# Full attention layers in 64x32 matmul tiles: two banks of values, two score tiles, values between the score pairs

## The chip, the cores and the metric

The kernel runs on one core of a Trainium2 chip. The metric is the device time of one execution in microseconds (us), the median of several runs. TensorE (PE, with its weight loads PEld) multiplies matrices into accumulation banks, VectorE (DVE), ScalarE (ACT) and GpSimd (POOL) work on rows of 128 partitions, SyncE (SP) issues transfers.

## What is computed

Four transformer layers without feed-forward parts, in the order A, B, A, B, each with layer norm and a residual sum. A is attention over a sliding window of 256, B is full attention. There are 2048 rows, 512 features, 32 heads of 16.

```python
qkv = (x @ wqkv).reshape(B, S, 3, H, Dh)          # B=1, S=2048, D=512, H=32, Dh=16
scores = einsum("bhqd,bhkd->bhqk", q, k) * Dh ** -0.5
# A only: where(0 <= i - j < 256, scores, -1e9)
o = einsum("bhqk,bhkd->bhqd", softmax(scores), v)
x = x + reshape(o) @ wo                            # x on the right is layer-normed first
```

## The kernel before

**Layers and loops.** Layers 0 and 2 are sliding layers, 1 and 3 full ones. `attention` goes over blocks of 512 queries (c, 4 of them) and over quarters of heads (qd, 8 quads of 4 heads); in this text one pass of `attn_full` over all keys for one c and qd is called a quarter. A quarter has 16 steps, one for each 128 keys (j). A full layer so has 32 quarters and 512 steps. In layer 3 the quarters come in the order of pairs of quads (t) first, then c.

**A step.** `exps` is called twice (pr 0 and 1). Each call makes the scores of two heads: two matmuls (L714) of 64 contraction rows (queries and keys lie there in float16 parts, with sums for the shift) by 128 key columns over 512 queries, into the two banks of a score tile. ScalarE then takes one exponential over both banks (L718, 128x1024), into one of six buffers `e`. Then `pv` of the step two before multiplies the exponentials by the values: four heads, each 128 rows by 17 columns (16 features and a column of ones, the denominator) in float32, written to the four 32-partition parts of one bank, `acc[0]` (L758). The compiled program has two matmul instructions for each of these.

**Score tiles.** The pool `ps_s` has two tiles of two banks. In full layers a third, `PH["third"]`, takes every third call.

**End of a quarter.** `epilogue` transposes the bank of values (VectorE, L686), keeps the least and the summed denominators, divides, and after every second quad transposes back and casts for the output projection (L689 to L702).

**Side work.** Projections of queries, keys and values, the output projection, and norms of later blocks run as generators (`Work`), in pieces of one 512-column matmul step (a "pass" below) between attention steps. The class `Side` hands them out: it keeps a modelled clock (`spent`), a budget per step (`share`), and a time `PH["free"]` before which no new tile is begun. A tile of side work is twelve passes (three in `wo_part`, layer 3), made by `mms`; in full layers each pass is four matmuls of 128 rows by 32 columns (L429) into one bank, `acc[1]`, which `bank()` returns. VectorE takes the result out of it: two operations for queries and keys (L527, L528), one for values (L638), one for output tiles (L652, L673). The squares of queries and keys are summed over heads by `squares` (L550) into the same bank and read by one operation. `finish` at the end of a block makes what is left, piece after piece.

**Order.** PE's instructions are issued in the order written (a manual schedule). The other engines' order is made by a scheduler with priorities (`high_priority` moves an instruction ahead). Values are queued in `pvq`; after each step `flush(2)` leaves two steps in it, then `sd.step()` gives the side its turn:

```python
pvq.append([f])
flush(2)
sd.step()
```

So PE's order in a step is: scores, scores, values of two steps before, side passes. Banks: two for `acc`, four for the score pool, two for the third tile, eight in all.

## Time and profile before

| | |
|---|---|
| runs | 2757.61 us median of 3 (2755.26 to 2764.16) |
| profiled execution | span 2759.8 us from first to last instruction; no other time is given for it |
| PE busy | 2636.2 us (96%) |
| ScalarE busy | 2377.0 us (86%) |
| VectorE busy | 956.6 us (35%) |
| GpSimd busy | 564.5 us (20%) |
| granted PE clock, mean | 0.992 |
| layer 1, layer 3 | 504 to 1456 us, 1789 to 2742 us (first to last exponential) |

How to read it. A row of groups has line, engine, operation, output and inputs by the program's names, count, then busy us, mean ns of one, and the engine's idle time before them with what ended it. A row of the timeline has start, length, engine, line, operation and count; a merged row covers several equal instructions. A row of stretches has start:end, length, and busy us (count) of PE, PEld, DVE, ACT and POOL, then granted clock, DMA share and GB/s. Matmuls are pipelined and their ends are modelled: distances of starts tell more than lengths. Slices of the page are a fortieth of the span each, digits are tenths.

### The profile page before, as it was taken

What the parts mean: (1) busy time and instruction counts of PE and PEld (TensorE: products, weight loads), DVE (VectorE), ACT (ScalarE), POOL (GpSimd) and SP (SyncE); (2) the same over time, 40 slices, a digit from 0 to 9 for tenths busy, and PEclk for the clock granted to TensorE, in tenths of its full rate; (3) what the DMA queues carried; (4) which work ended last, traced back from release to release, by engine and by line L of the source; (5) the groups of instructions that cost most, each with busy time, mean ns of one, the idle gap of its engine ahead of it and who ended that gap; (6) DMA issues with size and microseconds to landing.
All of it is one profiled execution on the core that took longest, in us unless ns stands there. A gap on an engine that the chain in (4) does not pass through costs nothing.

```text
span 2759.8 us, 59658 instructions
## 1 busy us (share of the span) xinstructions
PE 2636.2 (96%) x24358; PEld 782.5 (28%) x24358; DVE 956.6 (35%) x2059; ACT 2377.0 (86%) x2687; POOL 564.5 (20%) x1129
## 2 busy tenths in 40 slices
PE   8989999999999999999998898999999999999997
PEld 4333344322222222222223333522222222222221
DVE  7678765112131113112215676512222222222122
ACT  3566664799999999999995677399999999999997
POOL 2477672000000000000004677100000000000000
PEclk9999999999999999999999999999999999999999
DMA  6877676322232123212325464613333343333321
GB/s 222 218 251 222 197 229 186 123 71 88 86 102 88 62 82 108 85 60 91 103 67 177 146 190 131 184 62 105 110 112 122 120 123 101 102 110 114 98 95 56
DMA packets 317501, 344.78 MB, mean 125 GB/s; under 512 B 113056, under 2 KB 233376, under 8 KB 311200
## 3 DMA queue, kind: packets, MB, share of 16 engines
q1 hardware_dynamic: 317216, 340.86, 40.4%
q8 instruction: 193, 3.16, 0.5%
q14 instruction: 92, 0.75, 0.1%
HBM read 228.07 MB, written 96.99 MB: 118 GB/s over the span
## 4 chain that ended last, share of the span: by engine, by line
PE 74%; ACT 9%; DVE 6%; issue 5%; POOL 3%; DMA 3%; SPq 0%; ACTq 0%; DVEq 0%; POOLq 0%
PE acc L758 30%; PE s L714 19%; PE acc L429 10%; PE b L432 9%; ACT e L718 8%; PE acc L791 3%; PE bs L432 2%; POOL e L781 1%; DVE ot L686 1%; POOL e L784 1%; POOL wr L344 1%; DVE sp L528 0%; POOL w L346 0%; PE acc L550 0%; DMA kt<-kw 0%
## 5 line engine op out<-in xcount | busy, mean ns | idle before, releaser
L718 ACT ACTIVATE e<-s 128x1024 f32<-128x1024 f32 (+2 forms) x2432 | 2243.5, 1116 | 96.8 <-PE s L714 90.2
L758 PE MATMUL acc<-e,vt 128*17 128x512 f32 x8192 | 1078.0, 598 | 5.3 <-DVE ot L686 4.1
L714 PE MATMUL s<-qt,kt 64*128 64x512 f16 (+3 forms) x5504 | 780.5, 355 | 64.7 <-ACT e L718 41.8
L714 PEld LDWEIGHTS <-kt 64*128 64x128 f16 x5504 | 204.9, 94 | 818.1 <-issue 795.1
L784 POOL TENSOR_SCALAR_AFFINE_SELECT e<-e 128x256 f32<-128x256 f32 x512 | 226.5, 450 | 127.0 <-ACT e L718 126.4
L758 PEld LDWEIGHTS acc<-e,vt 128*17 128x17 f32 x8192 | 136.2, 95 | 379.5 <-issue 347.9
L686 DVE STREAM_TRANSPOSE ot<-acc 128x512 f32<-128x512 f32 x128 | 91.3, 714 | 387.9 <-PE acc L758 317.2
L702 POOL TENSOR_TENSOR oh<-o,oh 128x512 f16<-128x512 f32 x31 | 36.0, 1160 | 886.5 <-DVE oh L701 886.5
L781 POOL TENSOR_SCALAR_AFFINE_SELECT e<-e 128x256 f32<-128x256 f32 x448 | 197.7, 447 | 76.9 <-ACT e L718 74.8
L791 PE MATMUL acc<-e,vt 128*17 128x384 f32 (+2 forms) x2816 | 202.7, 394 | 6.0 <-POOL e L781 4.0
L432 PE MATMUL b<-xc,w 128*128 128x512 f16 x672 | 157.0, 384 | 8.4 <-DVE sp L528 6.9
L533 POOL TENSOR_TENSOR sq_h<-sp_h 128x512 bf16<-128x512 f16 x27 | 28.1, 1039 | 482.7 <-DVE sp_h L527 482.7
L527 DVE TENSOR_SCALAR sp<-acc,es 128x512 f16<-128x512 f32 x28 | 20.9, 748 | 288.5 <-PE acc L429 276.8
L527 DVE TENSOR_SCALAR sp_h<-acc,es 128x512 f16<-128x512 f32 x27 | 20.3, 751 | 286.5 <-PE acc L429 286.5
L525 ACT ACTIVATE sp<-b,es 128x512 f16<-128x512 f32 x56 | 38.5, 687 | 89.6 <-PE b L432 87.4
L429 PE MATMUL acc<-xc,w_h 128*32 128x512 f16 x1296 | 108.6, 379 | 2.3 <-DVE km L566 2.3
L533 POOL TENSOR_TENSOR sq<-sp 128x512 bf16<-128x512 f16 x28 | 29.1, 1039 | 396.5 <-DVE sp L527 396.5
L429 PE MATMUL acc<-xc,w 128*32 128x512 f16 x1344 | 108.9, 379 | 0.3
L638 DVE COPY vt<-acc 128x256 f32<-128x256 f32 (+1 forms) x36 | 18.5, 513 | 257.6 <-PE acc L429 257.6
L673 DVE TENSOR_TENSOR dx<-acc,gcol 128x512 f32<-128x512 f32 x60 | 41.5, 692 | 176.6 <-PE acc L429 176.6
L429 PE MATMUL acc<-wo,oh 128*32 128x512 f16 x1296 | 101.3, 379 | 0.0
L432 PEld LDWEIGHTS <-w 128*128 128x128 f16 x720 | 67.3, 99 | 105.6 <-issue 33.8
(167 smaller groups left out, 1808.2 us busy)
## 6 DMA issues: line engine op xcount, KB each, us to landing
kt<-kf SPq DMA_DIRECT2D x128, 512.0 KB
qt<-qs SPq DMA_DIRECT2D x128, 256.0 KB
xd<-x SPq DMA_DIRECT2D x96, 256.0 KB
x<-xd SPq DMA_DIRECT2D x96, 256.0 KB
w<-wd SPq DMA_DIRECT2D x20, 1024.0 KB
kt<-kw SPq DMA_DIRECT2D x64, 256.0 KB
qs<-sp SPq DMA_DIRECT2D x48, 256.0 KB
wo<-wd SPq DMA_DIRECT2D x12, 1024.0 KB
```

Source lines behind the costliest of these rows:

```text
L429: nc.tensor.matmul(ps[g:g + 32], a[:, g:g + 32], b, start=(i == 0), stop=(i == len(pairs) - 1), skip_group_check=True)
L432: nc.tensor.matmul(ps, a, b, start=(i == 0), stop=(i == len(pairs) - 1))
L527: nc.vector.tensor_scalar(sp[:, 0], ps, e, None, op0=ALU.mult)
L533: nc.gpsimd.tensor_tensor(sq, sp[:, 0], sp[:, 0], ALU.mult)
L673: nc.vector.tensor_tensor(d, ps, gcol[1], ALU.mult)
L686: nc.vector.transpose(ot.rearrange("p b r -> p (b r)"), a)
L714: nc.tensor.matmul(ps[:, h, s0:s0 + wd_], kt[R * h:R * h + R, pr, kc:kc + P], qt[R * h:R * h + R, pr, qc:qc + wd_], start=True, stop=True)
L718: nc.scalar.activation(e[:, :, w0:w1], ps[:, :, w0:w1], AF.Exp, scale=SCALE)
L758: nc.tensor.matmul(a[32 * h:32 * h + DH + 1, :], V[l, qd // 4, j // 8][:, j % 8, 4 * (qd % 4) + h, :], es_[h // 2][:, h % 2, :], start=(j ...
L781: nc.gpsimd.affine_select(v, v, pattern=[[0, 2], [-1, P]], compare_op=ALU.is_gt, fill=0.0, base=0, channel_multiplier=1)
L784: nc.gpsimd.affine_select(v, v, pattern=[[0, 2], [1, P]], compare_op=ALU.is_ge, fill=0.0, base=0, channel_multiplier=-1)
L791: nc.tensor.matmul(a[32 * h:32 * h + DH + 1, q * P:(q + nb) * P], V[l, (4 * c + j) // 4][:, j % 4, 4 * qd + h, :], es_[h // 2][:, h % 2, s ...
```

## The change

In full layers every matmul is made of tiles of 64 contraction rows by 32 columns.

- Scores: eight matmuls a pair instead of two, into the same two banks.
- Values: each head's 128 keys are split into two halves of 64, one into `acc[0]`, one into `acc[1]`; the epilogue transposes both banks and adds the halves.
- Side passes: the contraction is split into two halves, into the two banks of a tile `PH["pair"]`, which takes the banks of the third score tile. `joined` copies one half out and adds the other on VectorE; the old operations then read the sum. Values of the side work are joined at their destination.
- Score tiles: two.
- Order: values of two steps before are issued between a step's two score pairs, side passes after the second pair. In step 2 of each quarter, whose values are the first of the quarter, side passes come between the pairs and values at the end.
- The planner's modelled times for scores and values change (0.27 to 0.22, 1.0 to 0.88).

```diff
-    def bank():
+    def bank(halves=False):
         if PH["full"]:
-            return acc[1]
+            return PH["pair"] if halves else PH["pair"][:, 0, :]
...
                 for g in range(0, P, 32):
-                    nc.tensor.matmul(ps[g:g + 32], a[:, g:g + 32], b, start=(i == 0), stop=(i == len(pairs) - 1),
-                                     skip_group_check=True)
+                    for r in range(2):
+                        half = slice(R * r, R * r + R)
+                        nc.tensor.matmul(ps[g:g + 32, r], a[half, g:g + 32], b[half], start=(i == 0),
+                                         stop=(i == len(pairs) - 1), skip_group_check=True)
...
+    def joined(n, ps, rows=slice(0, P)):
+        if not PH["full"]:
+            return ps
+        j = vp.tile([P, QC], F32, name=f"j{n}", tag="dn", bufs=2)
+        with tc.high_priority(HEAD_START):
+            nc.vector.tensor_copy(j[rows], ps[rows, 0])
+            nc.vector.tensor_tensor(j[rows], ps[rows, 1], j[rows], ALU.add)
+        return j
...
+            ps = joined(f"{n}_{t}", ps)          # project; likewise in squares, wo, wo_part
...
+                if more is not None:             # values
+                    nc.vector.tensor_copy(to, more[:, part])
+                    nc.vector.tensor_tensor(to, fr, to, ALU.add)
...
             nc.vector.transpose(ot.rearrange("p b r -> p (b r)"), a)          # epilogue
+            if l % 2:
+                ou = vp.tile([P, QC // 32, 32], F32, name=f"ou{n}", tag="o", bufs=1)
+                nc.vector.transpose(ou.rearrange("p b r -> p (b r)"), acc[1])
+        if l % 2:
+            nc.vector.tensor_tensor(ot[:, :, :DH + 1], ot[:, :, :DH + 1], ou[:, :, :DH + 1], ALU.add)
...
-        ps = PH["third"] if PH["full"] and turn["s"] % 3 == 0 else ps_s.tile([P, 2, QC], F32, name=f"s{name}", tag="s")
+        ps = ps_s.tile([P, 2, QC], F32, name=f"s{name}", tag="s")
...
-            for h in range(2):
-                nc.tensor.matmul(ps[:, h, s0:s0 + wd_], kt[R * h:R * h + R, pr, kc:kc + P],
-                                 qt[R * h:R * h + R, pr, qc:qc + wd_], start=True, stop=True)
-        spent(0.27)
+            for g in range(0, P, 32 if PH["full"] else P):
+                for h in range(2):
+                    out_ = slice(g, g + 32) if PH["full"] else slice(0, P)
+                    nc.tensor.matmul(ps[out_, h, s0:s0 + wd_], kt[R * h:R * h + R, pr, kc + out_.start:kc + out_.stop],
+                                     qt[R * h:R * h + R, pr, qc:qc + wd_], start=True, stop=True,
+                                     skip_group_check=PH["full"])
+        spent(0.22 if PH["full"] else 0.27)
...
             for pr in range(2):                  # attn_full
+                if pr and j == 2:
+                    PH["side"]()
+                elif pr:
+                    flush(1)
                 es_.append(exps(f"{l}_{c}_{qd}_{j}_{pr}", kt[j // 8], qt, pr, [(j % 8 * P, 0, QC, 0)]))
...
                 for h in range(4):
-                    nc.tensor.matmul(a[32 * h:32 * h + DH + 1, :], V[l, qd // 4, j // 8][:, j % 8, 4 * (qd % 4) + h, :],
-                                     es_[h // 2][:, h % 2, :], start=(j == 0), stop=(j == NT - 1),
-                                     skip_group_check=True)
+                    for r in range(2):
+                        half = slice(R * r, R * r + R)
+                        nc.tensor.matmul(acc[r][32 * h:32 * h + DH + 1, :],
+                                         V[l, qd // 4, j // 8][half, j % 8, 4 * (qd % 4) + h, :],
+                                         es_[h // 2][half, h % 2, :], start=(j == 0), stop=(j == NT - 1),
+                                         skip_group_check=True)
+            if j == 2:
+                flush(1)
+            else:
+                PH["side"]()
             yield pv
...
                         pvq.append([f])          # attention
-                        flush(2)
-                        sd.step()
                         if win:
+                            flush(2)
+                            sd.step()
                             settle(False)
```

More of the change, by code (lines that the diff above doesn't have):

```diff
@@ L404, in phase @@
         PH["full"], PH["win"] = l is not None and l % 2 == 1, l is not None and l % 2 == 0
-        if PH["full"] or not PH["win"] and "pool" not in PH or l is None and PH.get("third"):
+        if PH["full"] or not PH["win"] and "pool" not in PH or l is None and PH.get("pair"):
             ps_x.close()
             PH["pool"] = ps_x.enter_context(tc.tile_pool(name=f"ps_x{l}", bufs=1 if PH["full"] else 2, space=bass.MemoryType.PSUM))
-            PH["third"] = PH["pool"].tile([P, 2, QC], F32, name=f"s{l}") if PH["full"] else None
-    def bank():
+            PH["pair"] = PH["pool"].tile([P, 2, QC], F32, name=f"s{l}") if PH["full"] else None
+    def bank(halves=False):
         if PH["full"]:
-            return acc[1]
+            return PH["pair"] if halves else PH["pair"][:, 0, :]
         turn["bank"] += 1
@@ L513, in project @@
         for t in range(NHT) if ht is None else (ht,):
-            ps = bank()
+            ps = bank(True)
             w0 = t * P if ht is None else 0
@@ L546, in squares @@
     def squares(n, sqs):
-        ph = bank()
+        ph = bank(True)
         for t, sq in sqs.items():
-            nc.tensor.matmul(ph[32 * t:32 * t + 32, :], hsum, sq, start=True, stop=True, skip_group_check=True)
-        return ph
+            if PH["full"]:
+                for r in range(2):
+                    half = slice(R * r, R * r + R)
+                    nc.tensor.matmul(ph[32 * t:32 * t + 32, r], hsum[half], sq[half], start=True, stop=True, skip_group_check=True)
+            else:
+                nc.tensor.matmul(ph[32 * t:32 * t + 32, :], hsum, sq, start=True, stop=True, skip_group_check=True)
+        return joined(n, ph, slice(0, P) if len(sqs) > 1 else quarters(*sqs))
     def quarters(ht):
@@ L623, in values @@
         for i in tiles:
-            ps = bank()[:, :D1 - D0]
+            ps = bank(True)
+            ps = ps[:, :, :D1 - D0] if PH["full"] else ps[:, :D1 - D0]
             if first:
@@ L628, in values @@
                 yield from mms(ps, [(xc[:, b, k, i * P:(i + 1) * P], w[:, k, a, :D1 - D0]) for k in range(NC) for a, b in TERMS], us=us)
-            src = ps.rearrange("p (h d) -> p h d", d=DH)
+            src, more = ((ps[:, r].rearrange("p (h d) -> p h d", d=DH) for r in range(2)) if PH["full"]
+                         else (ps.rearrange("p (h d) -> p h d", d=DH), None))
             for x, h in enumerate(halves if l % 2 else (None,)):
                 to = vt[:, i, :, :DH] if h is None else dst[h][:, i, :, :DH]
-                fr = src if h is None else src[:, x * HH:(x + 1) * HH]
-                if first:
+                part = slice(0, H) if h is None else slice(x * HH, (x + 1) * HH)
+                fr = src[:, part]
+                if more is not None:
+                    nc.vector.tensor_copy(to, more[:, part])
+                    nc.vector.tensor_tensor(to, fr, to, ALU.add)
+                elif first:
                     nc.vector.tensor_tensor(to, fr, first[2].rearrange("p (h d) -> p h d", d=DH), ALU.mult)
@@ L646, in wo @@
         for i in range(4):
-            ps = bank()
+            ps = bank(True)
             yield from mms(ps, [(O[l, c, t][:, a, i * P:(i + 1) * P], w[:, t, b, :]) for t in range(NHT) for a, b in TERMS])
@@ L650, in wo @@
             k = 4 * c + i
+            ps = joined(f"o{l}_{k}", ps)
             with tc.high_priority(HEAD_START):
@@ L667, in wo_part @@
         for i in range(4):
-            ps = bank()
+            ps = bank(True)
             yield from mms(ps, [(o[:, a, i * P:(i + 1) * P], w[:, b, :]) for a, b in TERMS])
@@ L672, in wo_part @@
             k = 4 * c + i
+            ps = joined(f"o3_{c}_{t}_{i}", ps)
             nc.vector.tensor_tensor(d, ps, gcol[1], ALU.mult)
@@ L722, in flush @@
         while len(pvq) > n:
-            spent(1.0)
+            spent(0.88 if PH["full"] else 1.0)
             for f in pvq.popleft():
@@ L757, in pv @@
                 for h in range(4):
-                    nc.tensor.matmul(a[32 * h:32 * h + DH + 1, :], V[l, qd // 4, j // 8][:, j % 8, 4 * (qd % 4) + h, :],
-                                     es_[h // 2][:, h % 2, :], start=(j == 0), stop=(j == NT - 1),
-                                     skip_group_check=True)
+                    for r in range(2):
+                        half = slice(R * r, R * r + R)
+                        nc.tensor.matmul(acc[r][32 * h:32 * h + DH + 1, :],
[4 more added lines that the diff above has]
+                flush(1)
+            else:
+                PH["side"]()
             yield pv
@@ L977, in attention @@
                     nxt = load(l, c, qd + 1) if qd + 1 in qds else None
-                    a = acc[qd % 2 if win else 0]
+                    a, PH["side"] = acc[qd % 2 if win else 0], sd.step
                     began = clock[0]
```

## The prediction

> **What bounds the kernel now.** I read the page first (engines and slices), then busy time by stretch, then the order of time inside the two full layers.

> ```profile
> span 2759.8 us, 59658 instructions
> PE 2636.2 (96%) x24358; PEld 782.5 (28%) x24358; DVE 956.6 (35%) x2059; ACT 2377.0 (86%) x2687; POOL 564.5 (20%) x1129
> PE   8989999999999999999998898999999999999997
> DVE  7678765112131113112215676512222222222122
> ACT  3566664799999999999995677399999999999997
> 504.00:1456.00 952.00, 941.27 (x9234) 224.14 (x9237) 184.26 (x426) 946.76 (x1024) 47.48 (x46) 1.00 0.27 83
> 1789.00:2742.00 953.00, 935.94 (x8761) 229.55 (x8759) 220.54 (x436) 944.96 (x1024) 45.44 (x42) 1.00 0.33 103
> ```

> The full layers are the two stretches of 952 and 953 us with 1024 exponentials each (512 steps of two). PE, VectorE and ScalarE stand there at 941, 184 and 947 us of 952: two engines are full, VectorE is four fifths idle. The sliding layers, the other 855 us, keep their instructions; the change cannot move them but at their ends. Which of the two full engines sets the pace is read from the order of time.

> ```profile
> 1076.05 0.92 PE L714 MATMUL s<-qt,kt 64*128 64x512 f16 x4
> 1076.89 1.05 PE L758 MATMUL acc<-e,vt 128*17 128x512 f32 x8
> 1077.88 0.92 PE L714 MATMUL s<-qt,kt 64*128 64x512 f16 x4
> 1079.71 0.92 PE L714 MATMUL s<-qt,kt 64*128 64x512 f16 x4
> 1161.38 0.60 PE L714 MATMUL s<-qt,kt 64*128 64x512 f16 x4
> 1161.92 1.05 PE L758 MATMUL acc<-e,vt 128*17 128x512 f32 x8
> 1162.79 0.61 PE L429 MATMUL acc<-wv,xc 128*32 128x512 f16 x8
> 1163.34 0.61 PE L714 MATMUL s<-qt,kt 64*128 64x512 f16 x4
> 1167.03 0.61 PE L714 MATMUL s<-qt,kt 64*128 64x512 f16 x4
> 1168.55 0.61 PE L714 MATMUL s<-qt,kt 64*128 64x512 f16 x4
> 1169.95 0.83 PE L429 MATMUL acc<-wv,xc 128*32 128x512 f16 x12
> 1170.71 0.61 PE L714 MATMUL s<-qt,kt 64*128 64x512 f16 x4
> ```

> Where no side work runs, score groups come every 1.83 us (1076.05, 1077.88, 1079.71) and PE waits inside them (0.84 us to the values, against 0.54 at 1161.38): this is ScalarE's own pace, 0.917 us for one exponential. Packed by PE, a step is 1.52 us without side passes (1167.03 to 1168.55), 1.96 with two (1161.38 to 1163.34), and a third adds 0.21 (0.76 from 1169.95 against 0.55 from 1162.79). So ScalarE is the floor, and PE passes it only in steps of two passes or more. The floor is 512 x 1.833 = 938.7 us a layer; the stretches hold 952 and 953, together some 27 over it, 2 of them first and last edges. **25 us is all that a faster PE can win.**

> **The parts.** Inside a step, scores to values cost 0.54 us where two 512-column pairs need 2 x 0.21, and the last pass to the next scores 0.34 (0.55 for two passes less 0.21): each of the two changes of tile shape costs 0.12 us or so. With all tiles 64x32 both go. PE then needs 2 x 0.21 + 0.87 (1161.92 to 1162.79) + 0.21 a pass: 1.71 with two passes, 0.12 under the floor. In the built order some 110 steps of three passes are left (1.92 us), mostly beside steps of none or one. So the 25 us may go, as far as nothing new comes.

> Work per instruction: a score pair becomes eight matmuls, a value group sixteen, a side pass eight; matmul instructions grow from 24,358 by about 26,000. Moved columns per tile stay 512, so if eight tiles run side by side as four do now, no stream gets longer. No row shows a 64x32 tile. The lower bound is 0: a pass of four tiles and a pair of two 64x128 tiles both take 0.21. The upper is 0.04 us a score pair, a third of a shape change. I take the lower, to which the rows of four tiles are nearest, and keep the upper for the range. The fetch of instructions doubles from a small share.

> ```profile
> q8 instruction: 193, 3.16, 0.5%
> L714 PEld LDWEIGHTS <-kt 64*128 64x128 f16 x5504 | 204.9, 94 | 818.1 <-issue 795.1 <-DMA kt<-kw 5.0 <-DMA qs<-sp_h 0.6
> 1162.36 0.12 PEld L429 LDWEIGHTS <-xc 128*32 128x32 f16 x4 [0.31 <-issue]
> ```

> Weight loads: a 128-column load takes 94 ns, and four 32-column loads stand in 0.12 us, so they run beside each other; I charge nothing. [...]

> **Two score tiles, values between the pairs.** ScalarE's chain through PE is now closed over two tiles.

> ```profile
> 1463.92 1.02 ACT L718 ACTIVATE e<-s 128x1024 f32<-128x1024 f32 x1
> 1464.99 0.34 PE L714 MATMUL s<-qt,kt 64*128 64x384 f16 x2 [0.43 <-ACT e L718]
> 1999.05 0.61 PE L429 MATMUL acc<-xc,w_h 128*32 128x512 f16 x8 [0.77 <-DVE km L566]
> 1999.59 0.61 PE L714 MATMUL s<-qt,kt 64*128 64x512 f16 x4
> 2000.09 3.89 ACT L718 ACTIVATE e<-s 128x1024 f32<-128x1024 f32 x4 [1.54 <-PE s L714]
> ```

> An exponential lasts 1.02 us unqueued, scores follow its end by 0.05 (1464.94 to 1464.99), an exponential follows the scores' start by 0.50. First pair, values, second pair: 0.05 + 0.21 + 0.87 + 0.50 + 1.02 = 2.65, and one more exponential, 0.917, gives 3.57 for two steps of 3.67. The spare is 0.1, where the third tile gave nearly a whole exponential. Normal steps still fit. At the end of a quarter the side passes go between the pairs of step 2 and the values after them, so two value groups stand round one score pair: 2 x (0.21 + 0.87) = 2.16 between the second pairs of steps 2 and 3, 0.33 over the floor. Of this the spare covers 0.1, and an earlier start up to 0.16 (the tile is free 0.97 after the exponential before, where PE usually comes at 1.13), less where side passes stand in between: 0.07 to 0.17 is left. I take 0.14, since nearly every step 2 has passes: 64 x 0.14 = 9 us (between 5 and 11). Each longer wait below also delays the other tile by 0.16 (1.08 from pair to pair, less 0.917), 25 times or 4 us, and I put the three-pass steps at 0.04 each, 4 us (0.09 over the floor, less what the spare leaves). Together 17 us.

> **VectorE, and who waits.** These rows price what it gets.

> ```profile
> L686 DVE STREAM_TRANSPOSE ot<-acc 128x512 f32<-128x512 f32 x128 | 91.3, 714 | 387.9 <-PE acc L758 317.2 <-PE acc L791 69.6
> L673 DVE TENSOR_TENSOR dx<-acc,gcol 128x512 f32<-128x512 f32 x60 | 41.5, 692 | 176.6 <-PE acc L429 176.6
> L638 DVE COPY vt<-acc 128x512 f32<-128x512 f32 x12 | 8.3, 692 | 128.2 <-PE acc L429 128.2
> L527 DVE TENSOR_SCALAR sp<-acc,es 128x512 f16<-128x512 f32 x28 | 20.9, 748 | 288.5 <-PE acc L429 276.8
> L528 DVE SCALAR_TENSOR_TENSOR sp<-acc,es,sp 128x512 f16<-128x512 f32 x28 | 21.0, 750 | 0.9
> 1069.15 0.72 DVE L686 STREAM_TRANSPOSE ot<-acc 128x512 f32<-128x512 f32 x1 [10.25 <-PE acc L758]
> 1069.92 0.13 PEld L758 LDWEIGHTS acc<-e,vt 128*17 128x17 f32 x8 [0.58 <-DVE ot L686]
> 1070.60 0.43 DVE L696 TENSOR_TENSOR op<-ot,r 128x256 f32<-128x256 f32 x1
> ...
> 1159.36 0.71 DVE L699 STREAM_TRANSPOSE o<-op 128x512 f32<-128x512 f32 x1
> 1160.11 0.43 DVE L701 CAST oh<-o 128x512 f16<-128x512 f32 x1
> ```

> VectorE gets a copy and an addition for each side tile (161 tiles, 2 x 0.69 us), one more addition for 36 value tiles, and a second transpose and a small addition for 64 quarters: about 310 us beside 405, still under 40% of the stretches. By share nothing is due. But the side bank is single, and the next tile's first pass waits for the joined copy with every score pair queued behind it, as the scores of 1999.59 stood behind the pass of 1999.05; so what counts is the place of each pair of operations in VectorE's queue. The bank of a value or output tile is now held for 1.4 us of VectorE instead of 0.69; that of a query or key tile for 1.4 instead of 1.5. And the quarter's closing chain (from 1069.15 to 1071.03 with even quarters, 1.14 more with odd ones for a transpose and a cast) grows by 0.72 for the second transpose and some 0.3 for its addition, to 4.1 us at most, in front of whatever tile ended meanwhile.

> I followed the two built orders (PE's and VectorE's) with these durations and marked where PE's next instruction is reached before VectorE is through:
> - A, a tile's evacuation behind a closing chain: 13 places. From one more operation than the step hides (0.3) to most of a chain (2.6), by where the tile ends; 1.15 in the mean: 15 us.
> - B, layer 3, where the planner closes a block and puts two tiles in one step: 6 places. The row at 2000.09 shows such a place now: 1.54 us without exponentials. With one or two VectorE operations of 0.69 more it is 2.2 to 2.9; 2.5 each: 15 us.
> - C, the first values of a quarter, which wait for two transposes (1.45 us instead of 0.72) with a tile's copy and addition before them: 6 places, 1.35 each: 8 us.

> In all other places the 1.8 us of a step hide both operations. Today PE waits for banks in few places, as ScalarE's idle time (last column) shows, first layer 1, then layer 3; so most of this is new.

> ```profile
> L718 ACT ACTIVATE e<-s 128x1024 f32<-128x1024 f32 x1024 | 946.9, 1078 | 3.8 <-PE s L714 2.8
> L718 ACT ACTIVATE e<-s 128x1024 f32<-128x1024 f32 x1024 | 945.0, 1207 | 7.0 <-PE s L714 5.4
> ```

> **Sum**, on the profiled span (the page gives no other time of this execution): 2759.8 - 25 + 17 + 15 + 15 + 8 = 2790. The span lies 2.2 us over the median of the three runs, within their 2755.3 to 2764.2, so the median after is about **2788 us**, 1.1% slower.

> [...]

> Moved with the rest: side passes now sit after the second pair, so their transfers leave the SP queue up to a step later; SP issues as many as before, and the keys of a quarter are asked for a quarter ahead. The planner's new prices (0.22, 0.88) only shift where side passes fall. Values keep their distance of two steps, so the six exponential buffers suffice.

> **Rivals.**
> 1. VectorE's waits vanish under the steps (its small operations overlap, or tiles end earlier than I place them). Then the floor is nearly reached: 2757.6 - 25 + 9 to 17 = 2742 to 2750, faster. For it: VectorE is 80% idle, and copies and additions have high priority. It decides where all new costs stay under 17 us. Against it: the bank is single, and the orders show the places. Chance 0.16.
> 2. Gains and waits cancel, 2757.6 within 8 us: A to C at 8 instead of 38. For it: places priced at their mean may partly be hidden. Chance 0.13.
> 3. Row halves of the float32 values do not run side by side. Then a value group takes 1.74 us, a step with 1.3 passes 2.43, 0.60 over the floor, and 1024 steps make some 3370 us. Nothing in the trace shows row halves with float32; the scores show them with float16 (four 64-row matmuls in 0.54). The change then does not do what it says. Chance 0.04.
> 4. Eight-tile groups cost 0.04 us a score pair: 0.08 a step uses up the spare, and the 110 three-pass and 64 closing steps lose it in full, 14 us; and VectorE's chains of 4 us run 10% longer at the 25 places, 10 us: 2812. With the closing steps at 11 and A at its longer half it is 2826, the upper end of my own case; its lower end is A to C at half and the closing steps at 5, 2765.

> **How the numbers follow.** Forecast (slower, 2766 to 2826, rival 4 in it) 0.67, rival 1 0.16, rival 2 0.13, rival 3 0.04. A difference of 0.3% (8.3 us) is about what a measurement can tell. Faster by more 0.16, within 0.13, slower 0.71. The range leaves out rival 3, the lower tip of rival 1 and the tails of the forecast: **2743 to 2826**.

> **What would show it.** Right: PE's score groups at 1.83 us nearly everywhere, no stretch at 1.96, no 0.1 us between scores and values; ScalarE's idle time grows from 10.8 us in both layers to over 30, behind side passes or first values that wait for VectorE's copy, addition or second transpose. Wrong: if ScalarE idles less than now (rival 1); if score groups come at over 1.85 us in stretches without any side pass (tile cost, or the two tiles do not close in 1.83); if a value group is over 1.0 us (rival 3).

## Result, and the profile after

The changed kernel takes **2820.26 us** (median of 4 runs, 2815.12 to 2824.82), the kernel before 2758.96 on the same chip: ratio 1.0223, 95% interval 1.0206 to 1.0240. It is 61 us slower where 30 were forecast: inside the range, near its upper end of 2826, with twice the forecast loss. The profiled execution is the slowest of the four (2824.82, its span 2823.1); against the 2759.8 of before it is 63.3 us longer.

The page of the changed kernel, its span, the first engine's row and the instruction queue (packets, MB, share):

```profile
span 2823.1 us, 112536 instructions
PE 2537.5 (90%) x50557; PEld 1121.1 (40%) x50557; DVE 1247.0 (44%) x2545; ACT 2385.4 (84%) x2687; POOL 592.1 (21%) x1129
q8 instruction: 397, 6.50, 1.0%
```

PE is busy 99 us less, and the kernel is longer. The full layers by stretch and by group (busy time of PE, weight loads, VectorE, ScalarE, GpSimd; then granted clock, DMA; in the groups busy time, mean ns, idle time before them), layer 1 first:

```profile
504.00:1469.50 965.50, 891.28 (x22494) 401.82 (x22499) 286.08 (x604) 948.67 (x1026) 60.27 (x46) 1.00 0.27 84
1802.60:2806.00 1003.40, 889.09 (x21648) 391.95 (x21645) 401.87 (x738) 953.27 (x1027) 58.54 (x42) 0.99 0.33 101
L752 ACT ACTIVATE e<-s 128x1024 f32<-128x1024 f32 x1024 | 948.4, 1063 | 15.7 <-PE s L747 14.2
L752 ACT ACTIVATE e<-s 128x1024 f32<-128x1024 f32 x1024 | 952.1, 1061 | 46.9 <-PE s L747 44.7
```

ScalarE's idle time in the two layers went from 10.8 to 62.6 us, 58.9 of it waits for scores. To see where, I took the spacing of the ends of the 1024 exponentials of each layer and summed what goes beyond ScalarE's own 0.917. This excess was 11.6 and 12.7 us before and is 24.9 and 59.4 now: 60.0 of the 63.3 us. All else, sliding layers and edges, holds 3.3.

PE's order of time at the place that the prediction read:

```profile
1161.12 0.41 PE L747 MATMUL s<-qt,kt 64*32 64x512 f16 x8
1161.34 1.05 PE L798 MATMUL acc<-e,vt 64*17 64x512 f32 x16
1162.19 0.41 PE L747 MATMUL s<-qt,kt 64*32 64x512 f16 x8
1162.41 0.41 PE L431 MATMUL s<-xc,w 64*32 64x512 f16 x8
1162.95 0.41 PE L747 MATMUL s<-qt,kt 64*32 64x512 f16 x8
...
1164.03 0.41 PE L747 MATMUL s<-qt,kt 64*32 64x512 f16 x8
1164.24 0.63 PE L431 MATMUL s<-xc,w 64*32 64x512 f16 x16
1164.79 0.41 PE L747 MATMUL s<-qt,kt 64*32 64x512 f16 x8
```

A pair costs 0.22, a value group 0.85, nothing lies between them; first pairs come 1.83 and 1.84 apart (1161.12, 1162.95, 1164.79), ScalarE's pace. The second of these steps has two passes, and such a step took 1.96 before. The change does to the matmuls what it says. The loss is in single places, and PE's waits name them (waited for: us in total, times, longest), first layer 1, then layer 3. PE's waits for a score tile that ScalarE still reads, 99.8 us in both layers, are not shown: there PE is ahead.

```profile
PE s L566 <- POOL sq L546: 4.2, 5, 1.3
PE s L431 <- DVE vt L656: 3.4, 4, 1.3
PE s L431 <- issue: 3.1, 3, 2.4
...
PE s L566 <- POOL sq_h L546: 17.1, 26, 2.3
PE s L431 <- DVE jk L450: 7.5, 8, 2.5
PE s L431 <- DVE jo L450: 6.1, 4, 1.5
PE s L431 <- issue: 3.3, 2, 1.9
PE acc L798 <- DVE ot L712: 2.3, 4, 0.7
```

The largest of these is one that the prediction does not have: matmuls on the squares (L566) that wait for GpSimd, 21.3 us against 2.7 before. The order of time at one of them:

```profile
2409.41 0.63 DVE L449 COPY j_h<-s 128x512 f32<-128x512 f32 x1
2410.28 0.69 DVE L450 TENSOR_TENSOR j_h<-s,j_h 128x512 f32<-128x512 f32 x1
2411.01 0.49 DVE L540 TENSOR_SCALAR sp_h<-j_h,es 128x512 f16<-128x512 f32 x1
2411.66 1.51 POOL L546 TENSOR_TENSOR sq_h<-sp_h 128x512 bf16<-128x512 f16 x1 [17.71 <-DVE sp_h L540]
2413.23 0.39 PE L566 MATMUL s<-sq_h,hsum 64*32 64x512 bf16 x2 [2.28 <-POOL sq_h L546]
2413.93 2.10 ACT L752 ACTIVATE e<-s 128x1024 f32<-128x1024 f32 x2 [1.83 <-PE s L747]
```

Copy, addition, scale and squares follow one another; PE reaches L566 2.28 us before the end, with every score pair queued behind it, and ScalarE stands idle for 1.83 us. Two further kinds were not foreseen. PE waits with no semaphore behind it ("issue"); and after some long waits it runs at half the clock (0.50 granted). The first, with the instruction queue's row for the stretch from 2251.6 to 2252.8:

```profile
2251.83 0.51 PE L431 MATMUL s<-wv,xc 64*32 64x256 f16 x16
2254.19 0.30 PE L431 MATMUL s<-wv,xc 64*32 64x256 f16 x8 [1.85 <-issue]
...
q8 instruction: 1, 0.02, 5.5%
```

PE stops in the middle of a value tile, whose operands have long been there, and goes on 2.45 us after a block of 16,384 bytes of instructions began to be read (2251.74 in the trace's record of that queue). All eight such places end in this way:

```
read begins   523.14  553.06  572.09  694.27 2066.30 2130.59 2186.26 2251.74
PE goes on    525.44  555.35  574.45  696.53 2068.78 2132.82 2188.82 2254.19
              2.30    2.29    2.36    2.26   2.48    2.23    2.56    2.45 us
```

The count of PE's matmuls and weight loads says the same. The queue made 397 reads for 101,114 of them, so some 255 a read; and counted in blocks of 256, all eight places have nearly the same remainder, 137 to 143 in layer 1 and 27 to 33 in layer 3. I read this as a wait for the block whose read had begun; the trace shows the times and the counts alone.

And the half clock, after a wait as long as the one above:

```profile
2349.91 0.61 PE L566 MATMUL s<-sq_h,hsum 64*32 64x512 bf16 x2 [2.28 <-POOL sq_h L546]
2350.32 2.33 PE L798 MATMUL acc<-e,vt 64*17 64x512 f32 x16
...
2349.90:2353.30 3.40, 3.39 (x52) 1.43 (x59) 2.07 (x3) 1.15 (x2) 0.00 (x0) 0.50 0.13 42
```

The value group takes 2.33 us instead of 1.05, the granted clock of the stretch is 0.50. The record of the clock shows four such stretches of 3.4 us in the full layers (from 574.9, 2025.6, 2349.9 and 2476.2 us), and none in the full layers of before. Their starts are 425, 95 and 37 times 3.413 us apart. With the trace divided into periods of 3.413 us from these starts, the four periods just before hold 2.23 to 2.52 us without a matmul, every other period of the full layers at most 1.93. Two more waits, 2.28 us at 2413.2 and 2.48 at 2283.5, are divided between two periods, and no half clock followed.

Every place with more than 0.25 us of excess, put to the wait of PE before it (small ones and the rest by difference). Of the 22 places of squares 14 cost only some 0.5 us each: the matmul on the squares is 0.3 to 0.5 late, and the next tile then waits 0.2 more for the join of its sums.

```
                                         predicted us (places)  measured us (places)
squares behind the join and GpSimd                0                 27.8 (22)
A  tile evacuation behind a closing chain        15 (13)             8.8 (8)
B  layer 3, two tiles in one step                15 (6)             20.2 (7)
C  first values behind two transposes             8 (6)              7.2 (5)
instructions that come late                       0                 11.7 (8)
closing steps, follow-ups, the rest              17                  8.6
sum                                              55                 84.3
```

The half clock is inside these rows. Twin places give its price: 3.73 and 3.76 us of excess with it against 2.53 without, behind the same wait of 2.28 (2349.9, 2475.3; 2413.2); 4.82 against 3.24 behind a wait of 2.47 and 2.48 (2025.8; 2283.5). With 1.2 for the fourth, an estimate after the first two, some 5 us.

### The profile page after: what moved, and what is told of

The parts are those of the page before. It is cut to its first block, busy times and chain, and to the rows that moved or that the text cites. A ratio compares the mean times of both kernels' runs of the same rounds, so it can differ in the third digit from the quotient of the medians.

```text
span 2823.1 us, 112536 instructions
## 1 busy us (share of the span) xinstructions
PE 2537.5 (90%) x50557; PEld 1121.1 (40%) x50557; DVE 1247.0 (44%) x2545; ACT 2385.4 (84%) x2687; POOL 592.1 (21%) x1129
## 4 chain that ended last, share of the span: by engine, by line
ACT 47%; PE 27%; issue 11%; DVE 9%; POOL 3%; DMA 2%; SPq 0%; ACTq 0%; POOLq 0%; DVEq 0%
ACT e L752 46%; PE b L434 9%; PE acc L798 5%; PE s L747 4%; PE acc L836 3%; PE s L431 3%; PE bs L434 2%; POOL sq_h L546 1%; POOL e L826 1%; POOL e L829 1%; DVE j_h L450 1%; DVE j_h L449 1%; POOL wr L344 0%; DVE ot L712 0%; DVE ou L715 0%
## 5 line engine op out<-in xcount | busy, mean ns | idle before, releaser
L747 PE MATMUL s<-qt,kt 64*32 64x512 f16 (+3 forms) x17792 | 992.1, 372 | 180.5 <-ACT e L752 140.6
L798 PE MATMUL acc<-e,vt 64*17 64x512 f32 x16384 | 1096.5, 590 | 4.4 <-DVE ot L712 2.7
L747 PEld LDWEIGHTS <-kt 64*32 64x32 f16 (+1 forms) x17792 | 457.3, 90 | 1074.0 <-issue 974.8
L798 PEld LDWEIGHTS acc<-e,vt 64*17 64x17 f32 x16384 | 288.3, 92 | 76.7 <-issue 8.5
L712 DVE STREAM_TRANSPOSE ot<-acc 128x512 f32<-128x512 f32 x128 | 91.3, 713 | 437.1 <-PE acc L798 366.6
L449 DVE COPY j_h<-s 128x512 f32<-128x512 f32 x27 | 18.5, 685 | 278.5 <-PE s L431 256.4
L449 DVE COPY jo<-s 128x512 f32<-128x512 f32 x72 | 49.8, 691 | 174.3 <-PE s L431 174.3
L431 PE MATMUL s<-xc,w_h 64*32 64x512 f16 x2592 | 113.3, 380 | 7.5 <-DVE jk L450 6.5
L431 PE MATMUL s<-wo,oh 64*32 64x512 f16 x2592 | 106.9, 379 | 10.3 <-DVE jo L450 6.5
L431 PE MATMUL s<-xc,w 64*32 64x512 f16 x2688 | 112.3, 376 | 3.2 <-DVE vt L656 1.7
L431 PE MATMUL s<-wv,xc 64*32 64x256 f16 (+1 forms) x3456 | 98.5, 305 | 10.3 <-issue 6.4
```

The lines of the kernel that those rows point to most:

```text
L431: nc.tensor.matmul(ps[g:g + 32, r], a[half, g:g + 32], b[half], start=(i == 0), stop=(i == len(pairs) - 1), skip_group_check=True)
L449: nc.vector.tensor_copy(j[rows], ps[rows, 0])
L712: nc.vector.transpose(ot.rearrange("p b r -> p (b r)"), a)
L747: nc.tensor.matmul(ps[out_, h, s0:s0 + wd_], kt[R * h:R * h + R, pr, kc + out_.start:kc + out_.stop], qt[R * h:R * h + R, pr, qc:qc + wd_] ...
L798: nc.tensor.matmul(acc[r][32 * h:32 * h + DH + 1, :], V[l, qd // 4, j // 8][half, j % 8, 4 * (qd % 4) + h, :], es_[h // 2][half, h % 2, :] ...
```

## Experiments

Theory 1 says that the small tiles are free and the loss is a set of places where PE reaches a bank, a square or an instruction too early. Theory 2 puts it to the tiles, to the two score tiles or to the mere number of instructions. Ratios are to the kernel before on the same chip, with 95% intervals; "excess" is the sum defined above, of the profiled run. Versions are compared with each other by medians from different chips, on which the kernel before takes 2759.0 to 2760.8 us.

**The tiles alone.** Before, with only the scores cut.

```
-            for h in range(2):
-                nc.tensor.matmul(ps[:, h, ...], kt[..., kc:kc + P], ...)
+            for g in range(0, P, 32 if PH["full"] else P):
+                for h in range(2):
+                    nc.tensor.matmul(ps[out_, h, ...], kt[..., kc + out_.start:kc + out_.stop], ...)
```

> The kernel before with one edit: the scores of the full layers are cut into 64x32 tiles (eight matmuls a pair instead of two). Values, side passes, three score tiles and order stay. Theory 1 (eight small tiles run side by side; what the changed kernel lost lies in the evacuation, not in the matmuls): score groups keep their time, no new wait on VectorE; if the change of shape is one of columns, a step loses 0.1 to 0.2 us of PE time and the 24 us over ScalarE's floor shrink, 2738 to 2750; if it is one of rows (64 against 128), nothing changes, 2755 to 2762. Theory 2 (each eight-tile pair costs PE more, or its 12,000 further matmul instructions do): packed steps grow, 2765 to 2800, with waits of PE that nothing releases.

Measured 2772.72, ratio 1.0038 (1.0027 to 1.0050): 11 us over the nearer range of theory 1, inside that of theory 2. PE's order of time:

```profile
1166.89 0.62 PE L716 MATMUL s<-qt,kt 64*32 64x512 f16 x16
1167.45 1.05 PE L761 MATMUL acc<-e,vt 128*17 128x512 f32 x8
1168.32 0.61 PE L429 MATMUL acc<-wv,xc 128*32 128x512 f16 x8
1168.86 0.62 PE L716 MATMUL s<-qt,kt 64*32 64x512 f16 x16
```

Scores to values is 0.56 instead of 0.54, and a step of two passes 1.97 instead of 1.95 (medians of all such steps). So an eight-tile pair costs some 0.01 us, a quarter of the prediction's upper bound, and the change of shape stays (0.12 of the 0.56, where two pairs take 0.44) although the scores are now 32 columns wide like the passes: it comes here with the 64 and 128 rows. The waits without a releaser that theory 2 asks for do not appear. The excess is 37.4 against 24.3, and 9 of these 13 us are excesses under 0.25 us, most of them in steps of two passes. With 1.33 passes in the mean the packed step goes from 1.81 to 1.825 of ScalarE's 1.83, so little is left for catching up after a long step; that this is the reason is argued and not shown.

**The order alone, and the tiles without it.** Before with two score tiles and the new order; the changed kernel with the old order.

```
two_tiles (on before):   + flush(1) or PH["side"]() between the pairs, side passes after the second pair
                         - the third score tile
old_order (on changed):  - flush(1) between the pairs;  flush(2) and sd.step() behind both pairs
```

> The kernel before with the changed order alone: two score tiles, the values between the pairs, side passes behind the second pair; all tile shapes, banks and evacuations as before. Theory 1 (waits behind the evacuation make the loss of the changed kernel): PE waits for ScalarE's two tiles, and the change of shape is now inside the closed chain (0.05 + 0.21 + 0.12 + 0.87 + 0.12 + 0.50 + 1.02 + 0.92 = 3.81 against 3.67 for two steps), so the step is up to 0.07 longer everywhere, 2775 to 2830, without any wait on VectorE's copies. Theory 2 (two tiles alone make the 61 us): 24 + 61 over before, about 2843 or more.

> The changed kernel with the order of before: both score pairs of a step, then the values of two steps ago and the side passes behind them. All tiles, banks and evacuations as changed, two score tiles. Theory 1 (the two tiles close only with the values between the pairs): behind the second pair stand 0.87 of values and 0.21 a pass, so the first pair of the next step starts 0.05 + 0.21 + 0.87 + 0.29 = 1.42 us after the exponential instead of 0.97, and its exponential 0.09 late with the mean of 1.33 passes, 0.3 with two, none without: some 0.1 to 0.15 a step, 2890 to 2980. Theory 2 (the order is worth little, the losses are all behind the evacuation): 2810 to 2840.

Measured 2957.01, ratio 1.0707 (1.0690 to 1.0725), by its number in theory 2's range; and 2976.02, ratio 1.0781 (1.0764 to 1.0797), in theory 1's. Two_tiles first, then old_order:

```profile
1230.29 0.39 PE L714 MATMUL s<-qt,kt 64*128 64x512 f16 x2
1230.61 1.05 PE L762 MATMUL acc<-e,vt 128*17 128x512 f32 x8
1231.60 0.39 PE L714 MATMUL s<-qt,kt 64*128 64x512 f16 x2
1231.92 0.40 PE L429 MATMUL acc<-wv,xc 128*32 128x512 f16 x4
1232.25 0.39 PE L714 MATMUL s<-qt,kt 64*128 64x512 f16 x2
...
1242.21 0.41 PE L747 MATMUL s<-qt,kt 64*32 64x512 f16 x8
1243.13 0.41 PE L747 MATMUL s<-qt,kt 64*32 64x512 f16 x8 [0.50 <-ACT e L752]
1243.34 1.05 PE L794 MATMUL acc<-e,vt 64*17 64x512 f32 x16
1244.20 0.84 PE L431 MATMUL s<-wv,xc 64*32 64x512 f16 x24
```

In two_tiles four changes of shape a step (0.11 each: 0.32 from a pair to what follows it, where the pair alone needs 0.21) make a step of one pass 1.96 us long (1230.29 to 1232.25), one of two 2.17 (to 1234.42). PE is the bound nearly everywhere (busy 977.7 of the 994.0 us from 506 to 1500), by 0.20 a step at 1.33 passes; 1024 times that is about the 196 us. I had counted the shape changes in the chain of the two tiles and not in PE's own sum, and so expected 130 less. The changed kernel has no such changes inside a step, so this loss is none of its 61 us. In old_order the second pair waits 0.50 for its tile, and values and passes then stand in front of the next pair; some 140 us of excess follow such waits. So order, two tiles and equal shapes belong together: neither half of the change works alone, and in the changed kernel the two tiles do close (8.6 us in the table).

**What the join costs.** The changed kernel without the second operation of the join; and without the second transpose.

```
one_half:       -  nc.vector.tensor_tensor(j[rows], ps[rows, 1], j[rows], ALU.add)   (and for the values)
one_transpose:  -  nc.vector.transpose(ou..., acc[1]);  - nc.vector.tensor_tensor(ot..., ou..., ALU.add)
```

> The changed kernel, without the additions that join the two row halves of side tiles: only the first bank is copied (a part of the sums is left out). VectorE's queue and the chain through GpSimd's squares get 0.69 us shorter at every side tile. Theory 1 (waits behind the evacuation): some 20 places of squares and some 12 of tile evacuations are each 0.5 to 0.69 shorter and those of 0.3 vanish; the slow clock after waits over 2.2 us vanishes at two of four places: 2790 to 2802. Theory 2 (instructions, tiles and score tiles make the loss): within 6 us of the changed kernel, 2815 to 2822.

> The changed kernel, with the quarter's closing chain as before: the second value bank is neither transposed nor added (its half of the value sums is left out). The chain gets 1.13 us shorter (0.68 + 0.45). Theory 1: the waits of first values for the transposes (5 places, 7 us) vanish, and waits of tiles and squares behind the chain get up to 1.1 shorter at some ten places: 2802 to 2812. Theory 2 (VectorE's queue is not what is late): within 4 us of the changed kernel.

Measured 2785.53, ratio 1.0087 (1.0069 to 1.0104): 35 us of 61 hang on the second operation of the join, 0.69 us of VectorE per tile, more than expected. And 2816.11, ratio 1.0197 (1.0179 to 1.0214): 4 us, about theory 2's value, with an interval that overlaps the changed kernel's. Waits in layer 3, one_half and then one_transpose:

```profile
PE s L565 <- POOL sq_h L545: 6.1, 5, 1.6
...
PE s L566 <- POOL sq_h L546: 15.3, 26, 1.6
```

Without the addition the waits for squares are 6 us at 5 places instead of 17 at 26. Without the second transpose they stay, since most squares do not lie behind a closing chain: the chain before the squares is the tile's own. The three longest, which do lie behind one, shrink from 2.28 to 1.57 us, but two of layer 1 grow to 2.74 and 2.75, for a reason not followed up. The five waits of first values keep their length, since they wait for the first transpose; with what follows they cost 4.3 us instead of 7.2.

**The squares.** On VectorE; and later.

```
squares_vector:  - nc.gpsimd.tensor_tensor(sq, sp[:, 0], sp[:, 0], ALU.mult)
                 + (nc.vector if PH["full"] else nc.gpsimd).tensor_tensor(sq, sp[:, 0], sp[:, 0], ALU.mult)
later_squares:   - PH["free"] = clock[0] + after
                 + PH["free"] = clock[0] + after + (1.8 if PH["full"] and after > 2 else 0)
                   least share of side work 0.33 and 0.34 -> 0.42
```

> The changed kernel with the squares of the full layers' projections on VectorE instead of GpSimd (1.51 us each there). Theory 1 (the matmuls on the squares wait for copy, addition, scale and GpSimd one behind the other): the waits of PE for the squares, 21 us in both full layers, fall to under 8, and the two 2.3 us ones no longer bring the half clock: 2796 to 2808. Theory 2 (VectorE's queue is what is late, so another operation there costs as much as GpSimd's share saves): 2815 to 2830, with longer waits behind the copies and additions.

> The changed kernel, where the next side tile, and so the matmuls on the squares of the tile before, comes 1.8 us later by the planner's clock after a projection tile (and the least share of side work per step is raised from 0.33 and 0.34 to 0.42, so that the work still ends in time). Theory 1 (the matmuls on the squares stand too near behind the join): their waits, 21 us in both full layers, fall under 6, and with them the half clock at two places: 2792 to 2806. Theory 2 (the distance doesn't matter, VectorE is late anyway): 2812 to 2825.

Measured 2812.88, ratio 1.0186 (1.0168 to 1.0204), and 2792.51, ratio 1.0112 (1.0095 to 1.0129). The matmuls on the squares in layer 3, squares_vector and then later_squares (idle time last):

```profile
L566 PE MATMUL s<-sq_h,hsum 64*32 64x512 bf16 x54 | 10.4, 377 | 8.4 <-DVE sq_h L546 8.4
L566 PE MATMUL s<-sq_h,hsum 64*32 64x512 bf16 x54 | 10.3, 376 | 0.6 <-POOL sq_h L546 0.6
```

VectorE squares in 0.42 us instead of 1.51, and half of the wait goes; the time falls by 7, less than the 12 to 24 expected, for neither theory. With more distance, and the larger least share that goes with it, the wait goes and the time falls by 28 us, as theory 1 had it: the squares were not slow, they were asked for too early. The 28 is a net figure. The squares' places, 27.8 us in the changed kernel, are all but gone, and late instructions cost some 5 us less; but waits behind copies of forced tiles grew (27 us of excess, 20.2 there), as the later tiles left more for the end of a block.

**The side tile alone.** The changed kernel with 128x32 side passes into one of the two banks in turn.

```
-    for r in range(2): nc.tensor.matmul(ps[g:g + 32, r], a[half, g:g + 32], b[half], ...)
+    nc.tensor.matmul(ps[g:g + 32], a[:, g:g + 32], b, ...)      bank: PH["pair"][:, turn, :], nothing joined
```

> The changed kernel, with side passes back in 128x32 tiles of one bank: the two banks of the side tile are used in turn, each tile is evacuated by one operation, nothing is joined. Scores and values stay in 64x32 tiles, the values in two banks, two score tiles, same order. Theory 1 (the loss sits in the joined side tiles): no wait of PE behind copies or additions and almost none for squares; the change of shape (0.11 each way) returns around side passes only; left are the closing steps, the first values behind two transposes (7 us) and the 24 us won: 2748 to 2775. Theory 2 (eight small tiles and two score tiles make the loss): 2795 or more.

Measured 2797.76, ratio 1.0135 (1.0118 to 1.0152), 23 us over the range that I gave theory 1 and inside theory 2's; the trace tells why:

```profile
1242.17 0.41 PE L741 MATMUL s<-qt,kt 64*32 64x512 f16 x8
1242.51 0.61 PE L430 MATMUL s<-xc,w 128*32 128x512 f16 x8
1243.05 0.41 PE L741 MATMUL s<-qt,kt 64*32 64x512 f16 x8
...
L563 PE MATMUL s<-sq_h,hsum 128*32 128x512 bf16 x27 | 10.5, 390 | 0.0
```

Its waits are as expected: none for squares, 8 us behind VectorE in both layers, none without a releaser. What I had not priced is that passes with two changes of shape (0.88 from pair to pair with two passes, 1242.17 to 1243.05, instead of 0.76) stand inside the closed chain of two tiles: excesses under 0.3 us sum to 48 us instead of 20. Of its excess of 62.1 that is the larger part, and it sits in the steps with two passes or more: in the mean 0.06 and 0.14 us in steps of two and three, against 0.00 and 0.03 in the changed kernel. So theory 1 holds for the joined tiles, whose waits are gone, and this version pays for it in the ring of two score tiles.

**Instructions.** The changed kernel, value passes of 2 x 128 columns instead of 256; part of the value sums is lost in this cut, while the data that go through PE stay the same.

```
+    for w in (slice(0, 128), slice(128, 256)):        # value tiles only
         nc.tensor.matmul(ps[g:g + 32, r, w], a[half, g:g + 32], b[half][:, w], ...)
```

> The changed kernel, with the passes of the 36 value side tiles cut into 128 columns instead of 256: twice the matmul instructions there (some 7,000 more in all), the same data through PE. Theory 1 (the waits of PE that no semaphore explains, 12 us at 8 places, are instructions that arrive late): such waits multiply in the value tiles, over 20 places, 2835 to 2890. Theory 2 (they come from something else): the passes only get a little longer, 2818 to 2830, and the waits without a releaser stay at 6 to 10.

Measured 2878.12, ratio 1.0431 (1.0410 to 1.0452). Waits of layer 3:

```profile
PE s L434 <- issue: 20.3, 13, 4.7
PE s L569 <- POOL sq_h L549: 17.0, 26, 2.3
```

Waits without a releaser give 66 us of excess at 26 places, instead of 11.7 at 8; the waits for squares stand as they were (17.0 against 17.1), and no other kind of place moved by more than 2 us. Each of the 35 waits ends 2.23 to 2.91 us after a read began, with the remainder of above (137 to 143, 27 to 37). Twice the instructions in these passes for the same data, and 66 us instead of 11.7: the number of instructions in a burst is the cause here.

**Repairs.** The changed kernel with a planner that keeps its distances; the kernel before with the part of it that concerns layer 3; and a second try.

```
repaired:         later squares; at most 4 passes a step; least share 0.42, 0.5;
                  O3 tiles left at a block's end go on in the next;
                  shift3: + if pend: yield "wait", pend[-1][0];   + PH["free"] = clock[0] + 3.4
before_repaired:  the last two lines, with 2.4
repaired_2:       left O3 tiles last in the blocks that hold shift3
```

> The changed kernel with a planner that knows of the join: later squares as in the run of that name, at most four side passes a step (fewer instructions in a burst), output tiles that are left at a block's end go on in the next block, and the key shift of layer 3 waits for its squares and holds the next tile back by 3.4 us. All tiles, banks and evacuations are those of the changed kernel. Theory 1 (the loss is places where PE comes too early to a bank, a square or an instruction): the waits behind copies and additions, 27 us with later squares alone, fall under 8, those of instructions under 5; left are the closing steps and first values: 2755 to 2772. Theory 2 (the join costs VectorE time that must surface somewhere): 2785 or more.

> The kernel before with the same repairs of layer 3's planner (output tiles go on in the next block, the key shift waits and holds the next tile back by 2.4 us), tiles as before. Tells what the repairs are worth without the change. Theory 1: the three places of 0.8 us behind the key maxima and their follow-ups go, 5 us: 2751 to 2757, so that the repaired change still doesn't pass it by much. Theory 2 (ScalarE's floor is reached already): 2757 to 2762.

> The repaired kernel, where output tiles left over from a block come last in the blocks that also hold the key shift and the next queries (in the repaired kernel those queries landed 5.2 us late once, 6.7 us of exponentials). Theory 1: that wait goes and nothing else moves: 2768 to 2775, still above the kernel before, because the closing steps and their follow-ups (20 us) have taken the place of the packed steps (16 us). Theory 2 (the losses come back in other places of the block): 2776 to 2785.

Measured 2778.17, ratio 1.0062 (1.0048 to 1.0076), 6 us over the range of theory 1 and under that of theory 2; 2757.11, ratio 0.9989 (0.9979 to 1.0000), no difference; and 2784.54, ratio 1.0084 (1.0071 to 1.0098), theory 2. (Part of layer 3's output comes out otherwise in repaired_2, for a reason that I did not look for; its time says no more than that the wait stayed.) The group of scores in repaired, both full layers and what lies between:

```profile
L748 PE MATMUL s<-qt,kt 64*32 64x512 f16 (+2 forms) x17088 | 919.7, 376 | 184.7 <-ACT e L753 154.2 <-DMA qt<-qs 5.1 <-DMA x<-xd 3.1
```

The excess of repaired is 38.1: 42 of the 61 us are back without a change of any tile or bank. PE's waits behind copies and additions are 5 us there and those for instructions 2, both as theory 1 had them, and none is left for squares. In the excess are 6.7 us behind one late load of queries (5.1 us of wait), which repaired_2 did not cure (12.9 there), and excesses under 0.3 us that sum to 19.5 against 16.4 before. Without that load 31 would be left, still over the 24.3 of before: what the packed steps cost then, closing steps, first values and some late instructions cost now. No version of the change beats the kernel before.

## Why the prediction was wrong

- **The bound.** Right. ScalarE's 0.917 per exponential is the floor, and the excess over it in before was 24.3 us by the exponentials' ends, 25 in the sum. Span less excess is 2733 to 2742 us in all fourteen kernels, before and changed among them: everything measured here is exponentials that come late.
- **Tiles and shapes.** Right: pairs of 0.22, value groups of 0.85, no switch inside a step, eight weight loads beside each other (all eight of a pair in 0.13 us at 1979.55). One after another, at the 94 ns of a load before, they would have taken 0.75 us. The lower bound for the eight-tile pair was nearly right (0.01 a pair in scores_64x32); rival 3 and rival 4's 0.04 are out. Two_tiles shows what four changes of shape a step cost, at 0.11 us each.
- **Two score tiles.** Too dear: 17 us in the sum, 8.6 by difference, with all that the table does not name.
- **A.** The step that failed is "In all other places the 1.8 us of a step hide both operations", with the list under it. I followed PE's and VectorE's orders and asked when a bank comes free. But of a query or key tile it is not the bank that is late, it is the squares: copy, addition and scale now run before GpSimd's 1.51 us, while the planner still lets the next tile, and with it the matmul on the squares, come 2.2 us of its clock after the last pass. The wait for squares had no term, and it cost 27.8 us. The closing chains of A were real but are not the whole: the copy at 2409.41 in the order shown above stands behind one, and so do those of 2349.9 and 2475.3, yet what PE waits for is the squares, at 2.5 to 3.8 us of excess where A took 1.15 in the mean. A by itself is 8.8 us against 15. Later_squares and one_half show the cause by intervention, 28 and 35 us, though neither acts on squares alone.
- **Instructions.** The sentence "The fetch of instructions doubles from a small share" was the second failure: 11.7 us, forecast none. The share of DMA time says nothing of a burst: a pass of 256 columns in a value tile takes 0.11 us by its starts, one of 512 columns 0.22, with eight matmuls each, so twice the instructions per us. In the full layers of before no wait of PE stands without a releaser, here eight do.
- **B and C.** Near in size: 20.2 against 15, of which 1.6 is the half clock and 2.4 a seventh place; 7.2 against 8.
- **The half clock.** Not in the sum: some 5 us, in four stretches of 3.4 us at a granted clock of 0.50. Before each of them PE had no matmul for 2.23 to 2.52 us of a period; in the full layers of before the most was 1.63, and no stretch was halved.
- **Rivals and signs.** The direction and the ground of it (VectorE's single waits, not shares) held: 35 of the 61 us hang on the second operation of the evacuation. None of the "wrong" signs came. The two mechanisms without a term cost 39.5 us; A and the two score tiles were 15 us too dear and B 5 too cheap, which makes the missed 30. That the time still lies in the range is luck: its upper end came from 0.04 us a score pair, dearer closing steps and longer waits of A, none of which came.

## What to carry to other kernels

When a tile's result comes in two banks, follow every consumer to its end and not to the release of the bank: here the matmul that needs the squared result, behind VectorE and GpSimd, was the dearest wait, and a planner's distances must be lengthened with the chain. Where a ring of buffers is cut from three to two to pay for faster matmuls, compare the gain with the engine that sets the floor first: 25 us were all there was, and the best repair stayed 17 us above the start. Cutting matmuls into more instructions cost little on average here (0.01 us a score pair) and much in bursts (11.7 us at eight places, 66 at 26 in wv_128); spread the short ones.
